# Filter coefficients by four small matmul tiles in one pair of PSUM banks, and folds issued half a step later

## The chip, the cores and the metric

The kernel runs on one core of one Trainium2 chip. The metric is the device time of one execution in microseconds (us); less is better. Five engines work side by side, each through its own queue in order: TensorE (PE; its weight loads are listed apart, as PEld), VectorE (DVE), ScalarE (ACT), GpSimd (POOL), and SyncE (SP), which here only issues DMAs. They wait for each other through semaphores.

## The reference

A long convolution by FFT gates the tokens, and two feed-forward layers follow:

```python
h_mlp = np.maximum(pos_emb @ w1, 0.0) @ w2          # filter: S x 64 -> 64 -> 128
u = x * v
h_filt = h_mlp * np.exp(-0.01 * pos)[:, None]
y = irfft(rfft(u, 2 * S) * rfft(h_filt, 2 * S))[:S]  # S = 12480, 128 channels
t = x * y
t = np.maximum(t @ moe_w_in, 0) ** 2 @ moe_w_out     # 128 -> 2048 -> 128
h = t @ moe2_w_in
out = (np.maximum(h, 0) + alpha * np.minimum(h, 0)) @ moe2_w_out
```

The change touches only how the filter's second layer (`@ w2`) is applied in the frequency domain and when its results are used.

## The kernel before, in words

The transform of length L = 110 x 229 is done as two small dense transforms, 110 points (`dfa`) and 229 points folded to 115 rows (`dfb`). The stages follow each other in program order, and a round-robin of Python generators (`run`) decides how two of them interleave. The order on each engine is the order in which this code issues.

- `z_stage`, `ar_stage`: first filter layer and its 110-point transform, kept in `ar` with 64 hidden features per frequency.
- `r_stage` with `u_stage(0)`: the 229-point transform of the 64 hidden features gives `r` tiles. One `r` tile is [128, 2, 4, 115]: on the 128 partitions lie 64 features of each of two frequencies, and it holds four frequencies in all (`q` = pair, then four combinations of real/imaginary and sign). Beside it, the first 64 channels of the signal are transformed into `U(0)`.
- **First half of the products** (`p_stage(0)`, 14 steps n = 0 to 13) beside `u_stage(1)`, which transforms the other 64 channels: `u_mm_a` (L312, 16 recorded passes per group of channels), `u_mm_b` (L320 to L325, 8 passes), and the **folds** (L328, two DVE instructions that add and subtract the two parts `pe` and `t`). `t` is an ACT copy of `po` (L324).
- **Second half of the products** (`p_stage(1)`, n = 14 to 27) beside `b_stage(0)`, the inverse transform of the first half (L409 on PE, L413 on ACT).
- Then `b_stage(1)`, `y_stage` (L466: inverse 110-point transform; two tiles of 64 output channels side by side in the array), and the two feed-forward layers, from about 313 us to the end.

One **step** n of `p_stage` does, for four frequencies: `filters(n, c)` for c = 0 (real) and c = 1 (imaginary): four matmuls each (L363) of the 128-partition `r` tile with a 128 x 128 block matrix `w2_sb` in which half of the entries are zero, so that both frequencies of a pair come out of one matmul. Each result has a bank of its own in turn (`r_h`, two banks). DVE multiplies it with U into A and then into B (L386; called **A** and **B** below). Then A is completed by a subtraction and an addition (L396, two instructions, on DVE, but on POOL in the steps of `on_pool` = 2, 6, 10, 15, 18, 21, 24, where B lies in SBUF and not in the PSUM tile `wide`), and POOL folds the result back into U (`finish`, L357). With two banks, PE may compute the next `filters(n + 1, 0)` as soon as A of step n has been read.

An fp32 matmul appears in the trace as two PE records, here called **passes**.

Of the kernel before, what the change touches and what calls it, by code (L numbers as in the profile page):

```python
# [58 lines left out]
def kernel(  # L59
# [18 lines left out]
    idft_o: bass.AP,  # L78
    out: bass.AP,
# [10 lines left out]
    six = [psum.tile([128, 512], F32, name=f"bank{i}") for i in range(6)]  # L90
    s_pair = ctx.enter_context(ExitStack())

    def last_two(name, *sizes):
        s_pair.close()
        pool = s_pair.enter_context(tc.tile_pool(name=name, bufs=1, space=PSUM))
        return [pool.tile([128, n], F32, name=f"{name}{i}") for i, n in enumerate(sizes)]

    banks = six + last_two("pair", 512, 512)
    r_any, r_six, r_a, r_b, r_h = Ring(banks), Ring(six), Ring(banks[0:2]), Ring(banks[2:5]), Ring(banks[5:8])
# [61 lines left out]
    def load_first(pool):  # L161
# [13 lines left out]
        nc.sync.dma_start(out=sig_sb, in_=sign)  # L175
        nc.sync.dma_start(out=dfa, in_=dft_a)
        load(3)
# [35 lines left out]
    def ar_stage():  # L213
# [7 lines left out]
        for c in range(F // 4):  # L221
            f0 = 4 * c
            p = [bank(r_six, HB, 4, K2) for s in range(2)]
            for s in range(2):
                for j in range(4):
                    nc.tensor.matmul(p[s][:, j], lhsT=rv[:, f0 + j, s], rhs=dfa[:, s * K2:(s + 1) * K2])  # L226
# [88 lines left out]
    def u_mm_b(k):  # L315
# [11 lines left out]
        for s, op in enumerate((ALU.add, ALU.subtract)):  # L327
            nc.vector.tensor_tensor(out=u[:, :, s], in0=pe, in1=t, op=op)  # L328
# [18 lines left out]
    def p_stage(h, t_ring, r_ring):  # L347
# [11 lines left out]
        def filters(n, c):  # L359
            H = bank(r_h, HB, DH, 2, 2, 2)  # L360
            for q in range(2):
                for s in range(2):
                    nc.tensor.matmul(  # L363
                        H[:, :, s, q], lhsT=r_t[p_order[n]][:, q, 2 * s + c], rhs=w2_sb[:, h * D:(h + 1) * D]
                    )
            return H

        first = []
        if h:
            first += [filters(nj, c) for c in range(2)]  # L370
            yield
        for n in range(h * nj, (h + 1) * nj):
# [379 lines left out]
    with tc.manual_schedule():  # L752
# [10 lines left out]
        with ExitStack() as st:  # L763
            late = st.enter_context(tc.tile_pool(name="late", bufs=1, side="right"))
            w2_sb = late.tile([128, 2 * D], F32, name="w2_sb")
# [3 lines left out]
            with tc.tile_pool(name="early", bufs=1) as early:  # L769
                run((z_stage(*load_first(early)), 1))  # L770
# [13 lines left out]
            (wide,) = last_two("wide", 1024)  # L784
            r_b.items, r_h.items, r_ab.items = six[2:4], six[4:6], six[0:4]
# [9 lines left out]
        banks = six + last_two("pair", 512, 512)  # L795
        r_y.items = six
# [87 lines left out]
def _tables(cell):  # L884
# [9 lines left out]
    ic[0] *= 0.5  # L894
    dft_b = np.zeros((HB, 3, HX), f)
# [8 lines left out]
    return w[cell].astype(f), dft_a, dft_b, e.astype(f), np.stack([o, -o], 1).astype(f)  # L904


def _arrays(inp):
    n, live, starts, order = _cells()
    cell, sign = _pairs(n, live)
    win, dft_a, dft_b, e, o = _tables(cell)  # L910
# [15 lines left out]
    w2 = np.zeros((2, F, 2, DH, 2), inp["w2"].dtype)  # L926
    for i in range(2):
        w1[i, :, i] = inp["w1"]
        w2[i, :, :, :, i] = inp["w2"].reshape(F, 2, DH)
# [34 lines left out]
```

## Time and profile before

| | us |
|---|---|
| time before, median of 3 runs (1384.39 to 1384.77) | 1384.49 |
| the profiled execution's own time | 1384.36 |
| its span, first to last instruction | 1382.6 |
| first half of the products (DVE's first A to its last B) | 119.1 to 186.5 |
| second half of the products | 195.2 to 241.1 |
| granted TensorE clock, mean over the span | 1.000 |

Over the whole span PE is recorded busy 99%, DVE 83%, POOL 74%, ACT 71%. PE's records overlap (they are modelled from issue to end), so what one pass costs is read from the distance of starts: the chain of waits gives it, as the time of a row divided by its count.

### The profile page before, as it was taken

What the parts mean: (1) busy time and instruction counts of PE and PEld (TensorE: products, weight loads), DVE (VectorE), ACT (ScalarE), POOL (GpSimd) and SP (SyncE); (2) the same over time, 40 slices, a digit from 0 to 9 for tenths busy, and PEclk for the clock granted to TensorE, in tenths of its full rate; (3) what the DMA queues carried; (4) which work ended last, traced back from release to release, by engine and by line L of the source; (5) the groups of instructions that cost most, each with busy time, mean ns of one, the idle gap of its engine ahead of it and who ended that gap; (6) DMA issues with size and microseconds to landing.
All of it is one profiled execution on the core that took longest, in us unless ns stands there. A gap on an engine that the chain in (4) does not pass through costs nothing.

```text
span 1382.6 us, 23568 instructions
## 1 busy us (share of the span) xinstructions
PE 1374.7 (99%) x8036; PEld 1193.9 (86%) x8036; DVE 1146.6 (83%) x1806; ACT 984.4 (71%) x1863; POOL 1029.3 (74%) x857
## 2 busy tenths in 40 slices
PE   9999999999999999999999999999999999999998
PEld 9999999998888888888888888888888888888898
DVE  6888989867888888888888878888888878888888
ACT  4453333638887777877777787778777787778777
POOL 4955969577877777777777777777777777777777
PEclk9999999999999999999999999999999999999999
DMA  8666423574000000000000000000000000000000
GB/s 250 185 199 186 129 65 114 157 245 146 31 2 0 9 9 1 8 9 8 9 9 9 8 1 9 9 8 8 9 8 1 9 8 8 9 9 9 1 8 19
DMA packets 59020, 66.27 MB, mean 48 GB/s; under 512 B 6226, under 2 KB 48019, under 8 KB 58771
## 3 DMA queue, kind: packets, MB, share of 16 engines
q1 hardware_dynamic: 58490, 64.56, 15.2%
q8 instruction: 63, 1.03, 0.3%
q14 instruction: 58, 0.48, 0.1%
q10 hardware_dynamic: 409, 0.21, 0.1%
HBM read 47.83 MB, written 16.92 MB: 47 GB/s over the span
## 4 chain that ended last, share of the span: by engine, by line
PE 96%; DVE 2%; issue 1%; POOL 1%; ACT 0%; POOLq 0%; DVEq 0%; ACTq 0%
PE bank L637 19%; PE bank L638 19%; PE bank L639 19%; PE pair L638 6%; PE pair L639 6%; PE pair L637 6%; PE bank L409 3%; PE bank L466 3%; PE bank L363 3%; PE bank L286 2%; PE bank L226 2%; PE bank L312 2%; PE bank L299 1%; PE pair L245 1%; PE bank L191 1%
## 5 line engine op out<-in xcount | busy, mean ns | idle before, releaser
L690 POOL TENSOR_TENSOR g<-R,g 128x512 fp32r<-128x512 f32 (+1 forms) x601 | 779.6, 1314 | 257.9 <-ACT g L679 243.7
L672 DVE SCALAR_TENSOR_TENSOR R<-bank,e 128x512 f32<-128x512 f32 (+1 forms) x800 | 530.8, 674 | 137.0 <-POOL g L690 99.2
L679 ACT CAST g<-R 128x512 fp32r<-128x512 f32 (+1 forms) x800 | 469.6, 605 | 76.6 <-DVE R L672 69.2
L657 ACT ACTIVATE e<-bank 128x512 f32<-128x512 f32 (+1 forms) x400 | 234.9, 587 | 104.0 <-PE bank L639 101.3
L662 DVE TENSOR_SCALAR e<-bank,alpha 128x512 f32<-128x512 f32 (+1 forms) x266 | 195.2, 734 | 35.9 <-PE bank L639 34.6
L690 DVE TENSOR_TENSOR g<-R,g 128x512 fp32r<-128x512 f32 (+1 forms) x199 | 185.0, 930 | 0.0
L638 PE MATMUL pair<-g,w_o 128*128 128x512 f32 (+1 forms) x400 | 153.7, 384 | 0.4 <-POOL g L690 0.4
L637 PE MATMUL bank<-x,w_i 128*128 128x512 f32 (+1 forms) x400 | 153.8, 385 | 0.0
L637 PE MATMUL pair<-g,w_o 128*128 128x512 f32 (+1 forms) x400 | 153.7, 384 | 0.0
L638 PE MATMUL bank<-x,w_i 128*128 128x512 f32 (+1 forms) x400 | 153.6, 384 | 0.0
L639 PE MATMUL bank<-x,w_i 128*128 128x512 f32 (+1 forms) x400 | 153.5, 384 | 0.0
L639 PE MATMUL pair<-g,w_o 128*128 128x512 f32 (+1 forms) x400 | 153.5, 384 | 0.0
L637 PE MATMUL bank<-g,w_o0b 128*128 128x512 f32 (+1 forms) x350 | 134.4, 384 | 0.0
L638 PE MATMUL bank<-g,w_o0b 128*128 128x512 f32 (+1 forms) x350 | 134.4, 384 | 0.0
L639 PE MATMUL bank<-g,w_o0b 128*128 128x512 f32 (+1 forms) x350 | 134.3, 384 | 0.0
L659 ACT ACTIVATE e<-bank 128x512 f32<-128x512 f32 (+1 forms) x134 | 78.8, 588 | 34.1 <-PE bank L639 32.5
L660 ACT ACTIVATE e<-e,alpha 128x512 f32<-128x512 f32 (+1 forms) x134 | 95.5, 713 | 4.4
L637 PEld LDWEIGHTS bank<-x,w_i 128*128 128x128 f32 x400 | 75.1, 188 | 15.0 <-DVE R L672 0.9
L638 PEld LDWEIGHTS pair<-g,w_o 128*128 128x128 f32 x400 | 75.1, 188 | 14.7 <-POOL g L690 1.0
L639 PEld LDWEIGHTS bank<-x,w_i 128*128 128x128 f32 x400 | 75.1, 188 | 14.4
L639 PEld LDWEIGHTS pair<-g,w_o 128*128 128x128 f32 x400 | 75.1, 188 | 14.4
L638 PEld LDWEIGHTS bank<-x,w_i 128*128 128x128 f32 x400 | 75.3, 188 | 13.8
(138 smaller groups left out, 2531.9 us busy)
## 6 DMA issues: line engine op xcount, KB each, us to landing
r<-spill SPq DMA_DIRECT2D x22, 460.0 KB, 3.3
G<-in_xs_dram SPq DMA_DIRECT2D x32, 224.0 KB, 3.8
G<-in_vs_dram SPq DMA_DIRECT2D x32, 224.0 KB, 3.7
spill<-r SPq DMA_DIRECT2D x14, 460.0 KB, 3.0
out_dram<-R SPq DMA_DIRECT2D x23, 256.0 KB, 2.0
s_w<-in_moe_w_out_dram SPq DMA_DIRECT2D x16, 256.0 KB, 5.3
s_w<-in_moe_w_in_dram SPq DMA_DIRECT2D x16, 256.0 KB, 2.9
w_spill<-w_o SPq DMA_DIRECT2D x15, 256.0 KB, 4.2
```

The costliest lines, as they stand in the source:

```text
L363: nc.tensor.matmul(H[:, :, s, q], lhsT=r_t[p_order[n]][:, q, 2 * s + c], rhs=w2_sb[:, h * D:(h + 1) * D])
L409: nc.tensor.matmul(p[:, d], lhsT=U(h, 2 * (x0 + d) + e, 1)[:, 0], rhs=icosb if e == 0 else isinb)
L637: nc.tensor.matmul(p, lhsT=wl, rhs=xh, start=first, stop=False)
L638: nc.tensor.matmul(p, lhsT=wh, rhs=xl, start=False, stop=False)
L639: nc.tensor.matmul(p, lhsT=wh, rhs=xh, start=False, stop=last)
L657: nc.scalar.activation(out=r, in_=p, func=ACTF.Relu)
L659: nc.scalar.activation(out=r, in_=p, func=ACTF.Relu, scale=-1.0)
L660: nc.scalar.activation(out=r, in_=r, func=ACTF.Copy, scale=alpha[:, t:t + 1])
L662: nc.vector.tensor_scalar(out=r, in0=p, scalar1=0.0, scalar2=alpha[:, t:t + 1], op0=ALU.min, op1=ALU.mult)
L672: nc.vector.scalar_tensor_tensor(out=g, in0=p, scalar=0.0, in1=r, op0=ALU.max, op1=op)
L679: nc.scalar.copy(out=gh, in_=g)
L690: eng.tensor_tensor(out=gl, in0=g, in1=gh.bitcast(F32), op=ALU.subtract)
```

## The change

**Filters.** `w2_sb` holds the 64 x 128 matrix twice, once per half of the partitions, with no zeros. Each old matmul (128 rows, 115 columns of weights, 128 moving columns) becomes four: 64 rows (one frequency of the pair), 64 or 51 columns of weights (the 115 output rows cut at 64), 64 moving columns. A step has 32 of them instead of 8, all issued together in `filters(n)`. The results of a step, both c, lie in one tile `filt` of two banks, one bank per frequency of the pair. `filt` exists once: `filters(n + 1)` is issued after A and B of step n, and writes where they read.

**Reading.** DVE reads `filt` with a step of 256 elements between the four frequencies of a channel (before: four neighbours). PE writes every second element. To give the pairs the right members, the 110-point transform of the filter has its own table `dff` with permuted columns, loaded early, with the first signal loads ahead of `dfa`.

**Folds.** `u_mm_b` returns its folds, and `u_stage` issues them after the next `u_mm_a`. The counts given to `run` change a little.

**Banks.** Four fixed PSUM banks and four regrouped ones instead of six and two.

```diff
-        def filters(n, c):
-            H = bank(r_h, HB, DH, 2, 2, 2)
+        def filters(n):
+            k, w = n // nj * DH, r_t[p_order[n]]
+            H = filt.rearrange("p (r q c d s) -> p r q c d s", r=2, q=2, c=2, s=2)
             for q in range(2):
                 for s in range(2):
-                    nc.tensor.matmul(
-                        H[:, :, s, q], lhsT=r_t[p_order[n]][:, q, 2 * s + c], rhs=w2_sb[:, h * D:(h + 1) * D]
-                    )
-            return H
-
-        first = []
-        if h:
-            first += [filters(nj, c) for c in range(2)]
-            yield
+                    for c in range(2):
+                        for r in range(2):
+                            f = slice(F * r, F * r + F)
+                            for b in (slice(0, 64), slice(64, HB)):
+                                nc.tensor.matmul(H[b, r, q, c, :, s], lhsT=w[f, q, 2 * s + c, b], rhs=w2_sb[f, k:k + DH])
+
+        hv = filt[:HB].rearrange("p (k c x) -> p c x k", k=4, c=2)
+        if not h:
+            filters(0)
...
             for c, out_c in enumerate((A, B)):
-                H = first.pop(0) if first else filters(n, c)
-                hv = H.rearrange("p d s q r -> p (d s) (q r)")
...
-                        in1=hv[:, x0:x0 + m].unsqueeze(2).to_broadcast([HB, m, 2, 4]),
+                        in1=hv[:, c, x0:x0 + m].unsqueeze(2).to_broadcast([HB, m, 2, 4]),
...
                 if c == 0:
                     yield
+            if n + 1 < 2 * nj:
+                filters(n + 1)
             for c, op in ((0, ALU.subtract), (1, ALU.add)):
...
     def u_stage(h, parts=None):
+        folds = None
         for k in range(h * NG, (h + 1) * NG + 1):
             if k < (h + 1) * NG:
                 prep(min(k + NV - 3, loaded[0] - 1))
                 load(k + NV - 1)
                 u_mm_a3(k, parts) if parts else u_mm_a(k)
+            if folds:
+                folds()
+            if k < (h + 1) * NG:
                 yield
             if k > h * NG:
-                u_mm_b3(k - 1) if parts else u_mm_b(k - 1)
+                folds = u_mm_b3(k - 1) if parts else u_mm_b(k - 1)
+                if folds and k == (h + 1) * NG:
+                    folds()
                 yield
...
-            run((some(u, 2 * NG - 1), 2 * NG), (p0, 2 * nj + 3))
-            next(q0)
+            run((some(u, 2 * NG - 1), 2 * NG), (p0, 2 * nj + 1))
             next(u)
             next(back)
-            run((b_stage(0, False), NG), (q0, 2 * nj + 3))
+            run((b_stage(0, False), NG), (q0, 2 * nj + 2))
```

Before, PE in the second half, `bank_73` and `bank_74` being the two filter banks and `bank_69` to `bank_72` those of the inverse transform:

```order
L363 MATMUL bank_73<-w_sb,r_112 115x64x2 x4
L363 MATMUL bank_74<-w_sb,r_112 115x64x2 x4
L409 MATMUL bank_71<-dfb,G 112x116 x4
L409 MATMUL bank_72<-dfb,G 112x116 x4
L363 MATMUL bank_73<-w_sb,r_110 115x64x2 x4
```

The same place now, where `wide_1134` is the tile `filt`:

```order
L422 MATMUL bank_70<-dfb,G 112x116 x4
L380 MATMUL wide_1134<-w_sb,r_112 64x64
L380 MATMUL wide_1134<-w_sb,r_112 51x64
...
L422 MATMUL bank_71<-dfb,G 112x116 x4
L422 MATMUL bank_72<-dfb,G 112x116 x4
```

The two groups of four became one run of 32, of which the first matmul waits for DVE and the rest for nothing.

Before, DVE at the start of the first half (`T` is A, or both A and B in an `on_pool` step; L328 are the folds), steps 1 to 3:

```order
L328 TENSOR_TENSOR R_82<-bank_71,G 115x4x112 x2
L386 TENSOR_TENSOR T_1137<-G,bank_73 115x128
L386 TENSOR_TENSOR T_1137<-G,bank_73 115x896
L386 TENSOR_TENSOR wide_1132<-G,bank_74 115x128
L386 TENSOR_TENSOR wide_1132<-G,bank_74 115x896
L396 TENSOR_TENSOR T_1137<-T_1137,wide_1132 115x128x4 x2
L328 TENSOR_TENSOR R_82<-bank_71,G 115x4x112 x2
L386 TENSOR_TENSOR T_1139<-G,bank_73 115x128
```

The same place now (`wide_1135` is the old `wide`):

```order
L397 TENSOR_TENSOR T_1140<-G,wide_1134 115x128
L397 TENSOR_TENSOR T_1140<-G,wide_1134 115x896
L332 TENSOR_TENSOR R_82<-bank_71,G 115x4x112 x2
L397 TENSOR_TENSOR wide_1135<-G,wide_1134 115x128
L397 TENSOR_TENSOR wide_1135<-G,wide_1134 115x896
L409 TENSOR_TENSOR T_1140<-T_1140,wide_1135 115x128x4 x2
L397 TENSOR_TENSOR T_1142<-G,wide_1134 115x128
```

The folds moved from behind L396 to between A and B; that is so in steps 1 to 4 and 10 to 13. In steps 4 to 9 a pair of folds stands behind B (and L396), as before.

Before, DVE in the second half:

```order
L386 TENSOR_TENSOR T_1136<-R_82,bank_73 115x1024
L386 TENSOR_TENSOR wide_1132<-R_82,bank_74 115x1024
L396 TENSOR_TENSOR T_1136<-T_1136,wide_1132 115x128x4 x2
L386 TENSOR_TENSOR T_1137<-R_82,bank_73 115x1024
L386 TENSOR_TENSOR wide_1132<-R_82,bank_74 115x1024
```

The same place now:

```order
L397 TENSOR_TENSOR T_1139<-R_82,wide_1134 115x1024
L397 TENSOR_TENSOR wide_1135<-R_82,wide_1134 115x1024
L409 TENSOR_TENSOR T_1139<-T_1139,wide_1135 115x128x4 x2
L397 TENSOR_TENSOR T_1140<-R_82,wide_1134 115x1024
L397 TENSOR_TENSOR wide_1135<-R_82,wide_1134 115x1024
```

The order is the same; what moved is the bank: every multiplication reads the one tile `wide_1134`.

## Rows read from the trace of the kernel before

**Rows 1.** Windows of the span: start:end, length, busy of engines (instructions), clock, DMA
```profile
118.20:188.90 70.70, 70.31 (x579) 68.76 (x577) 64.35 (x106) 24.00 (x45) 60.19 (x75) 1.00 0.43 128
193.50:243.30 49.80, 48.68 (x466) 48.26 (x464) 47.08 (x52) 17.63 (x33) 42.05 (x34) 1.00 0.39 118
```

**Rows 2.** Chain that ended last: start, length, what; one step of the first half
```profile
169.49 0.88 PE bank L363 x8
170.37 0.38 PE bank L320 x2
170.75 0.38 PE bank L321 x2
171.13 0.38 PE bank L322 x2
171.50 0.38 PE bank L325 x2
171.88 0.87 PE bank L363 x8
172.76 1.61 PE bank L312 x16
```

**Rows 3.** The same chain: a step of the second half, a handover to DVE, the stage behind
```profile
203.87 1.75 PE bank L363 x16
205.62 1.59 PE bank L409 x16
...
231.46 0.03 issue
231.48 0.02 DVEq L386
231.50 0.04 issue
...
243.29 25.61 PE bank L409 x256
```

**Rows 4.** Windows, DVE alone: first half, between the halves, second half
```profile
119.10:186.50 67.40, 61.99 (x102) 1.00 0.44 130
186.50:195.10 8.60, 4.70 (x9) 1.00 0.19 56
195.10:241.10 46.00, 43.78 (x46) 1.00 0.36 106
```

**Rows 5.** Timeline of DVE: start, length, line; two places of the first half
```profile
125.35 1.27 DVE L386 TENSOR_TENSOR T<-G,bank 115x128 f32<-115x128 f32 x2
126.54 1.42 DVE L386 TENSOR_TENSOR wide<-G,bank 115x128 f32<-115x128 f32 x2
127.99 1.29 DVE L396 TENSOR_TENSOR T<-T,wide 115x512 f32<-115x512 f32 x2
129.20 1.15 DVE L328 TENSOR_TENSOR R<-bank,G 115x448 f32<-115x448 f32 x2
130.26 2.47 DVE L386 TENSOR_TENSOR T<-G,bank 115x128 f32<-115x128 f32 x4
133.13 1.16 DVE L328 TENSOR_TENSOR R<-bank,G 115x448 f32<-115x448 f32 x2 [0.39 <-ACT G L324]
```

**Rows 6.** Timeline of DVE: one step of the second half
```profile
195.16 1.22 DVE L386 TENSOR_TENSOR T<-R,bank 115x1024 f32<-115x1024 f32 x1
196.30 1.22 DVE L386 TENSOR_TENSOR wide<-R,bank 115x1024 f32<-115x1024 f32 x1
197.55 1.29 DVE L396 TENSOR_TENSOR T<-T,wide 115x512 f32<-115x512 f32 x2
198.75 2.35 DVE L386 TENSOR_TENSOR T<-R,bank 115x1024 f32<-115x1024 f32 x2
```

**Rows 7.** PE's filter passes: two bursts on the timeline, the first one held up by DVE
```profile
200.13 2.16 PE L363 MATMUL bank<-w_sb,r 128*115 128x128 f32 x16
...
203.71 1.91 PE L363 MATMUL bank<-w_sb,r 128*115 128x128 f32 x16
```

**Rows 8.** PE in the y stage, window of L466 alone: length, busy (passes)
```profile
271.00:311.00 40.00, 40.00 (x852) 1.00 0.81 252
```

**Rows 9.** Timeline of PE at the start of the y stage
```profile
269.13 0.83 PE L445 MATMUL bank<-w_i 128*128 128x112 f32 x6
269.90 0.33 PE L466 MATMUL bank<-ide,G 112*64 112x55 f32 x4
270.06 0.31 PE L466 MATMUL bank<-ido,G 112*64 112x55 f32 x3
270.18 0.27 PE L466 MATMUL bank<-ide,G 112*64 112x110 f32 x1
270.21 0.22 PE L466 MATMUL bank<-ido,G 112*64 112x55 f32 x1
```

**Rows 10.** Groups by line: count, busy us, mean ns, idle before; ACT's copy, DVE's strided read
```profile
L324 ACT COPY G<-bank 115x448 f32<-115x448 f32 x14 | 7.5, 533 | 20.6 <-PE bank L322 20.6
...
L228 DVE COPY R<-bank 115x448 f32<-115x448 f32 x16 | 10.0, 624 | 4.4 <-PE bank L226 4.2
...
L328 DVE TENSOR_TENSOR R<-bank,G 115x448 f32<-115x448 f32 x32 | 18.4, 617 | 4.9 <-ACT G L324 4.9
```

More of the change, by code (lines that the diff above doesn't have):

```diff
@@ L78 @@
     idft_o: bass.AP,
+    dft_f: bass.AP,
     out: bass.AP,
@@ L89, with last_four @@
     psum = ctx.enter_context(tc.tile_pool(name="psum", bufs=1, space=PSUM))
[L90 to L95, printed above, removed]
+    four = [psum.tile([128, 512], F32, name=f"bank{i}") for i in range(4)]
+    s_four = ctx.enter_context(ExitStack())
+    def last_four(name, *sizes):
+        s_four.close()
+        pool = s_four.enter_context(tc.tile_pool(name=name, bufs=1, space=PSUM))
         return [pool.tile([128, n], F32, name=f"{name}{i}") for i, n in enumerate(sizes)]
-    banks = six + last_two("pair", 512, 512)
-    r_any, r_six, r_a, r_b, r_h = Ring(banks), Ring(six), Ring(banks[0:2]), Ring(banks[2:5]), Ring(banks[5:8])
+    banks = four + last_four("lone", 512, 512, 512, 512)
+    r_any, r_six, r_a, r_b, r_h = Ring(banks), Ring(banks[:6]), Ring(banks[0:2]), Ring(banks[2:5]), Ring(banks[5:8])
     r_ab, r_y = Ring([]), Ring([])
@@ L175, in load_first @@
         nc.sync.dma_start(out=sig_sb, in_=sign)
+        nc.sync.dma_start(out=dff, in_=dft_f)
+        load(3)
         nc.sync.dma_start(out=dfa, in_=dft_a)
-        load(3)
         nc.sync.dma_start(out=dfb, in_=dft_b)
@@ L225, in ar_stage @@
                 for j in range(4):
-                    nc.tensor.matmul(p[s][:, j], lhsT=rv[:, f0 + j, s], rhs=dfa[:, s * K2:(s + 1) * K2])
+                    nc.tensor.matmul(p[s][:, j], lhsT=rv[:, f0 + j, s], rhs=dff[:, s])
             for s, copy in enumerate((nc.scalar.copy, nc.vector.tensor_copy)):
@@ L326, in u_mm_b, with folds @@
         u = U(h, 2 * DG * g, 2 * DG).rearrange("p (d s) (c k) -> p d s c k", s=2, c=2)
-        for s, op in enumerate((ALU.add, ALU.subtract)):
-            nc.vector.tensor_tensor(out=u[:, :, s], in0=pe, in1=t, op=op)
+        def folds():
+            for s, op in enumerate((ALU.add, ALU.subtract)):
+                nc.vector.tensor_tensor(out=u[:, :, s], in0=pe, in1=t, op=op)
+        return folds
     def u_stage(h, parts=None):
+        folds = None
         for k in range(h * NG, (h + 1) * NG + 1):
@@ L764 @@
             late = st.enter_context(tc.tile_pool(name="late", bufs=1, side="right"))
-            w2_sb = late.tile([128, 2 * D], F32, name="w2_sb")
+            w2_sb = late.tile([128, D], F32, name="w2_sb")
             dfa = late.tile([NA, 2 * K2 + KA], F32, name="dfa")
@@ L769 @@
             with tc.tile_pool(name="early", bufs=1) as early:
+                dff = early.tile([NA, 2, K2], F32, name="dff")
                 run((z_stage(*load_first(early)), 1))
@@ L789 @@
             u = u_stage(1)
-            run((some(u, 2 * NG - 1), 2 * NG), (p0, 2 * nj + 3))
-            next(q0)
+            run((some(u, 2 * NG - 1), 2 * NG), (p0, 2 * nj + 1))
             next(u)
             next(back)
-            run((b_stage(0, False), NG), (q0, 2 * nj + 3))
-        banks = six + last_two("pair", 512, 512)
-        r_y.items = six
+            run((b_stage(0, False), NG), (q0, 2 * nj + 2))
+        banks = four + last_four("apart", 512, 512, 512, 512)
+        r_y.items = banks[:6]
         wa = ctx.enter_context(tc.tile_pool(name="wa", bufs=1))
@@ L941, in _arrays @@
         arrays[k] = a.view(np.int64) if a.dtype.itemsize == 8 else a
-    arrays.update(win=win, sign=sign, dft_a=dft_a, dft_b=dft_b, idft_e=e, idft_o=o)
+    arrays.update(win=win, sign=sign, dft_a=dft_a, dft_b=dft_b, idft_e=e, idft_o=o, dft_f=dft_f)
     return arrays, starts, order
```

14 lines of the change are left out of this document (7 added, 7 removed).

## Prediction

> **What bounds the kernel now.** I read the windows of the two halves of the products first. In both PE is busy all the time and DVE nearly so: 64.35 of 70.7 us and 47.08 of 49.8 us [rows 1]. The chain of waits runs over PE in both, and its rows give the price of a step. First half: 0.88 + 1.52 + 0.87 + 1.61 = 4.88 us, of which 1.75 are the 16 filter passes [rows 2]. Second half: 1.75 + 1.59 = 3.34 us [rows 3]. Then I read DVE's timeline for its price of the same step. First half: A 1.19 (start to start), B 1.45, L396 1.21, folds 1.06, together 4.91 us, or 3.70 where L396 lies on POOL [rows 5]. Second half: A and B 2.39, L396 1.20, together 3.59 [rows 6]; without L396 some 2.36. So PE and DVE are within a few per cent of each other, and what lets both run is that each has something in hand: with a bank for each of the two results, PE computes the next filters while DVE still multiplies. DVE is idle for only 67.40 - 61.99 = 5.4 us in the first half and 46.00 - 43.78 = 2.2 us in the second [rows 4]. Behind the products PE alone is the bound (25.61 us of L409 without a gap [rows 3], then the y stage and the layers), so a delay of the products reaches the end undiminished.
>
> **What a burst of 32 small matmuls takes.** No row shows a tile of 64 rows and 64 columns. One pass by itself is bounded by its weights or its moving columns: L312 takes 1.61/16 = 101 ns for 115 weight columns (0.875 ns each), L363 1.75/16 = 109 ns for 128 moving columns (0.855 ns each) [rows 2, 3]. For 64 and 64 that is 55 to 56 ns; I take 58, with 2 ns for the handing over. A step has 64 passes, 16 on each of the four tiles. If the tiles work side by side, the burst takes 16 x 0.058 = 0.93 us; if nothing overlaps, 64 x 0.058 = 3.7 us. The nearest row is the y stage, with two tiles of 64 columns: 852 passes in 40 us are 46.9 ns each [rows 8], while one of 110 moving columns needs 94 ns, so both tiles work at full rate. I take 0.93 us: a gain for PE of 0.8 us per step, 23 us over 28 steps.
>
> **What it does to the path.** The gain falls on an engine that no longer sets the end. The burst of step n + 1 may start only when B of step n has been read, and A of step n + 1 only when the whole burst is done. From the end of B to the next A, DVE cannot multiply for a time G:
> - PE's restart after a wait: the burst that DVE held up took 2.16 us, the next one 1.91 [rows 7]: 0.25.
> - Fifteen passes to the start of the last one: 15 x 0.058 = 0.87.
> - The record of the last pass, some 0.24 (0.22 to 0.27 in the y stage [rows 9]), and 0.09 until DVE runs [rows 3].
>
> G = 1.46 us (0.25 of the restart may shrink, so 1.2 to 1.5). Only L396 and folds can fill it.
>
> Second half: each of 14 steps takes 2.39 + 1.46 = 3.85 us; L396 (1.20) fits into G where it is on DVE, and nothing fills it in the four steps where it is on POOL. From the first A to the last B: 13 x 3.85 + 2.36 = 52.4 us, against 241.1 - 195.2 = 45.9: **+6.5 us**. PE needs only 1.59 + 0.93 + 0.3 of the 3.85.
>
> First half: DVE's work is the same, so I count its idle time. Behind steps 0, 1, 3, 11, 12 stands L396 alone: 5 x (1.46 - 1.21) = 1.25. Behind steps 2 and 10 (on POOL) nothing: 2.92. Behind step 6 a pair of folds: 0.40. Behind 5, 7, 8, 9 L396 and folds, 2.27: nothing. The moved folds cost, too. In eight steps they stand between A and B, and they need `u_mm_b`, which on PE now stands behind the burst: after the start of the burst's last pass (1.12 after B) come its stream and a change of the array's shape, 0.15 (L466 starts 0.20 after the last L445, whose passes are 0.11 apart [rows 9]), three matmuls of 0.38 [rows 2], 0.2 for the record's end and the signal, ACT's copy 0.53 [rows 10] and 0.1: 3.25 us after B. A is through at 1.46 + 1.19 = 2.65, so DVE waits 0.6 each time: 4.8. Behind step 4 the fold stands in the gap itself and waits for the same chain: 3.25 - 1.21 = 2.0. Together 11.4, less the 5.4 of before: **+6.0 us**. Before, such folds waited at times (0.39 [rows 5]).
>
> Between the halves DVE idles 8.60 - 4.70 = 3.9 us now [rows 4], waiting for the last folds; the two that remain there wait 2.0 and some 1.8: nothing. The first A waits for a burst of 0.93 instead of one of 0.88, plus a change of shape: +0.2.
>
> Edits taken at nothing: the stride of DVE's reads (L228 reads a bank at a stride of 112 elements in 624 ns, the folds neighbours in 617 [rows 10]; 7 ns on 56 multiplications would be 0.4 us), the two PSUM splits (the same number of banks in every ring outside the products), `dff` (smaller than `dfa`, in its place; `dfa` is first used behind the whole `ar` stage, which hides its later load), POOL (its work is unchanged, and a longer step gives it more room), `w2` (half the bytes). PE's writes at every second element have no row; if they slowed a pass to the old 109 ns, the burst would take 1.75 us, which is the first rival's price.
>
> Sum: 6.5 + 6.0 + 0.2 = 12.7 us. Against the profiled execution, 1384.36 (0.1 below the median), this gives **1397 us**.
>
> **Rivals.**
> 1. *Two tiles at a time.* The two passes of an fp32 matmul go to the same tile one behind the other, so if PE starts passes strictly in order, the next tile can overlap only with the second pass: the burst takes 64 x 0.058 / 2 = 1.86 us, and G 2.39. Second half 13 x 4.78 + 2.36 = 64.5 (+18.6). First half 5 x 1.18 + 4.8 + 1.33 + 2.9 + 0.5 + 4.8 = 20.2 (+14.8). With the 0.2 and a longer first burst +34, 1418 us. Against it: at the start of the y stage a 110-column pass of the next group starts at 270.18, ahead of a 55-column pass of the group before at 270.21 [rows 9], so tiles run out of order. For it: only two tiles were ever seen. The Trainium skill states the order as a rule ("TensorE: Matmul & The Clock Gate", Part 3, What overlaps and what doesn't: matmuls start and end strictly in program order); the row just named disagrees, by 0.03 us at one place. The same page (Part 1, on the 56 ns) gives a floor of about 25 ns from start to start; by an estimate from it, 64 passes take 1.6 us, and the time would be some 1412; no run here shows passes closer than 46.9 ns on average.
> 2. *The tiles do not overlap at all*, and the change only adds passes: burst 3.7 us, G 4.2. Second half 13 x 6.6 + 2.4 = 88 (+42), first half +39: 1466 us. The y stage speaks against it.
> 3. *A shorter burst.* If both passes of a matmul overlapped as well, or weights of 64 rows loaded faster, the burst were some 0.45 us and G 0.98, less than L396. Second half 9 x 3.59 + 4 x 3.37 + 2.4 = 48 (+2.3), first half 2.0 + 1.5 + 4.8 - 5.4 (+2.9): 1390 us. No row has a pass below its columns' price.
> 4. *Not slower: the multiplications get shorter.* They read the filters from two banks instead of one (L386, now L397); if that made them faster, 56 of them pay for 12.7 us at 0.23 us each (of some 1.2), and at 0.18 the change is within 0.2%: 1384 to 1387. L228 and the folds, one strided and one not, read at the same rate, so there is no sign of it.
>
> **How the numbers follow.** Forecast (1393 to 1402, with G from 1.25 to 1.65): 0.61. Two at a time, or a floor between (1405 to 1423): 0.23. No overlap: 0.05. Short burst (1388 to 1391): 0.06. Shorter multiplications: 0.05. The range that leaves out no more than 2 in 10 runs from 1389 to 1421. About 0.2% (2.8 us) is what a measurement of this kernel can tell from no change. Slower by more: 0.61 + 0.23 + 0.05 + 0.06, less 0.02 for short bursts that end within it: 0.93. Within: 0.05. Faster: 0.02.
>
> **What would show it.** The window of the second half: PE's share falls to some 70%, and DVE's idle time grows from 2.2 to 8 or 9 us, put down to PE's filter line; the distance from one A to the next is 3.85 us in steps with and without L396 alike. Passes of the filter line: 64 in about 0.93 us (1.86 in the first rival, 3.7 in the second). In the first half DVE's folds wait for ACT in steps 1 to 4 and 10 to 13. The y stage starts some 13 us later than 269.9, and from there all is as before. The forecast is wrong if A of the next step starts less than 1.2 us after B where L396 is on POOL, if multiplications no longer take 1.2 us, or if the stages before 118 us or behind 313 us change their length.

## The result, and the profile of the changed kernel

The changed kernel takes **1396.71 us** (median of 4 runs, 1395.81 to 1397.09), the kernel before 1384.47 beside it on the same chip: a ratio of 1.0088, 95% interval 1.0073 to 1.0102. It is slower by about 12 us. Its profiled execution took 1397.09 us, with a span of 1395.3.

The windows of after that answer to [rows 1, 4], from the first A to the last B of a half and of the time between (columns: start:end, length, then busy us and instructions of PE, PE's weight loads, DVE, ACT, POOL, then the granted clock, DMA share and GB/s):

```profile
120.54:195.22 74.68, 62.85 (x1184) 57.61 (x1184) 64.02 (x104) 23.42 (x44) 59.29 (x72) 1.00 0.40 118
195.22:202.53 7.31, 6.42 (x96) 5.38 (x96) 3.60 (x7) 1.06 (x2) 2.76 (x4) 1.00 0.18 64
202.53:253.90 51.37, 40.36 (x1067) 37.32 (x1067) 44.58 (x46) 16.25 (x30) 41.91 (x34) 1.00 0.33 96
```

The first half grew from 67.40 to 74.68 us, the second from 46.00 to 51.37; between them 8.60 became 7.31. PE is now idle for 11.8 us in the first and 11.0 in the second, where it was busy nearly all the time, and DVE's idle time grew too: 10.7 us instead of 5.4, and 6.8 instead of 2.2. The two engines, which had worked at the same time throughout, now work by turns for the length of each burst.

DVE's timeline in the second half (start, length, line; in brackets its idle time before and what ended it) beside [rows 6]:

```profile
203.66 1.22 DVE L397 TENSOR_TENSOR wide<-R,wide 115x1024 f32<-115x1024 f32 x1
204.92 1.29 DVE L409 TENSOR_TENSOR T<-T,wide 115x512 f32<-115x512 f32 x2
206.24 2.35 DVE L397 TENSOR_TENSOR T<-R,wide 115x1024 f32<-115x1024 f32 x2
209.94 1.22 DVE L397 TENSOR_TENSOR T<-R,wide 115x1024 f32<-115x1024 f32 x1 [1.35 <-PE wide L380]
```

and PE's in the same place:

```profile
204.94 1.15 PE L380 MATMUL wide<-w_sb,r 64*64 64x64 f32 x64 [2.36 <-DVE wide L397]
206.03 1.84 PE L422 MATMUL bank<-dfb,G 115*112 115x116 f32 x16
208.65 1.16 PE L380 MATMUL wide<-w_sb,r 64*64 64x64 f32 x64 [0.78 <-DVE T L397]
```

B of a step ends at 204.88, PE starts the burst at 204.94, and the next A starts at 206.24: the gap is 1.36 us, and L409 lies in it from 204.92 to 206.21. At 208.59 the same gap stands bare, because L409 lies on POOL: 1.35 us idle, put down to PE's filter line L380. A follows A after 3.71 us in both cases (202.53, 206.24, 209.94), with L409 or without. Before, it was 3.59 with it and 2.36 without.

In the first half a step looks like this on DVE, where [rows 5] had the folds behind L396:

```profile
124.45 1.28 DVE L397 TENSOR_TENSOR T<-G,wide 115x128 f32<-115x128 f32 x2
126.34 1.16 DVE L332 TENSOR_TENSOR R<-bank,G 115x448 f32<-115x448 f32 x2 [0.61 <-ACT G L326]
127.42 1.42 DVE L397 TENSOR_TENSOR wide<-G,wide 115x128 f32<-115x128 f32 x2
128.87 1.29 DVE L409 TENSOR_TENSOR T<-T,wide 115x512 f32<-115x512 f32 x2
130.12 1.29 DVE L397 TENSOR_TENSOR T<-G,wide 115x128 f32<-115x128 f32 x2
```

The folds stand between A and B and wait 0.61 us for ACT's copy. A step takes 5.67 us instead of 4.91. The view of the waits from 117 to 275 us adds it up (us, times, longest):

```profile
DVE T L397 <- PE wide L380: 10.9, 8, 2.1
DVE R L332 <- ACT G L326: 10.1, 11, 1.9
```

From the last B to the y stage nothing changed. It starts 28.81 us after it in both, at 282.69 us (PE's timeline, below) instead of 269.90 [rows 9]:

```profile
282.69 0.33 PE L479 MATMUL apart<-ide,G 112*64 112x55 f32 x4
```

### The profile page after: what moved, and what is told of

It is laid out like the page before. It is cut to its first block, busy times and chain, and to the rows that moved or that the text cites. A ratio compares the mean times of both kernels' runs of the same rounds, so it can differ in the third digit from the quotient of the medians.

```text
span 1395.3 us, 26237 instructions
## 1 busy us (share of the span) xinstructions
PE 1362.8 (98%) x9380; PEld 1174.2 (84%) x9380; DVE 1147.2 (82%) x1806; ACT 983.2 (70%) x1863; POOL 1028.7 (74%) x857
## 4 chain that ended last, share of the span: by engine, by line
PE 91%; DVE 6%; issue 1%; ACT 1%; POOL 1%; DMA 0%; SPq 0%; POOLq 0%; ACTq 0%; DVEq 0%
PE bank L650 13%; PE bank L651 13%; PE bank L652 13%; PE apart L650 13%; PE apart L651 13%; PE apart L652 12%; DVE T L397 2%; PE bank L479 2%; DVE wide L397 2%; PE bank L288 2%; PE lone L247 2%; PE bank L422 2%; PE wide L380 1%; PE bank L228 1%; DVE R L332 1%; DVE T L409 1%
## 5 line engine op out<-in xcount | busy, mean ns | idle before, releaser
L651 PE MATMUL apart<-g,w_o 128*128 128x512 f32 (+1 forms) x400 | 153.7, 384 | 0.4 <-POOL g L703 0.4
L650 PE MATMUL bank<-x,w_i 128*128 128x512 f32 (+1 forms) x400 | 153.8, 385 | 0.0
L650 PE MATMUL apart<-g,w_o 128*128 128x512 f32 (+1 forms) x400 | 153.7, 384 | 0.0
L652 PE MATMUL apart<-g,w_o 128*128 128x512 f32 (+1 forms) x400 | 153.5, 384 | 0.0
L650 PE MATMUL apart<-g,w_o0b 128*128 128x512 f32 (+1 forms) x350 | 134.4, 384 | 0.0
L651 PE MATMUL apart<-g,w_o0b 128*128 128x512 f32 (+1 forms) x350 | 134.4, 384 | 0.0
L652 PE MATMUL apart<-g,w_o0b 128*128 128x512 f32 (+1 forms) x350 | 134.3, 384 | 0.0
L651 PEld LDWEIGHTS apart<-g,w_o 128*128 128x128 f32 x400 | 75.1, 188 | 14.7 <-POOL g L703 1.0
L652 PEld LDWEIGHTS apart<-g,w_o 128*128 128x128 f32 x400 | 75.1, 188 | 14.5
```

What stands on the lines that cost most here:

```text
L650: nc.tensor.matmul(p, lhsT=wl, rhs=xh, start=first, stop=False)
L651: nc.tensor.matmul(p, lhsT=wh, rhs=xl, start=False, stop=False)
L652: nc.tensor.matmul(p, lhsT=wh, rhs=xh, start=False, stop=last)
```

## The experiments

Times are compared with runs of the kernel before on the same chip (1384.3 to 1384.6 us). All but one start from the changed kernel or from one another. Of each edit the lines that matter are shown; `...` marks what is left out. The question of the first seven is what the 12 us are made of; of the other five, whether the loss belongs to the small tiles or only to the place of their burst, and what is left of the change when the burst is out of the way.

**The fold move, undone.** In `u_mm_b`, the folds are issued at once:

```diff
-        return folds
+        folds()
```

> The changed kernel with the folds of u_mm_b issued at once again, as before the change; tiles, banks and the place of the filter bursts stay. Theory: on PE the three u_mm_b matmuls now stand behind the burst, so the folds are ready only some 3.25 us after B; placed at once they stand ahead of the next A, and DVE waits for the whole chain in the gap (3.25 + 1.06 us) where after waits 1.36 and then 0.6 between A and B: some 1.3 to 1.7 us more in each of 13 steps of the first half, 1413 to 1420 us, second half unchanged (51.35 us from first A to last B). Rival: the moved folds are themselves a cost (the 4.8 us of waits in the middle of eight steps), and undoing them gives some 1390 to 1393. A move worth nothing gives 1396.7.

Measured: 1428.2 us (1426.9 to 1431.83), ratio 1.0319 (1.0304 to 1.0335). DVE's timeline, an early and a late place, and the window between:

```profile
125.25 1.16 DVE L332 TENSOR_TENSOR R<-bank,G 115x448 f32<-115x448 f32 x2 [1.86 <-ACT G L326]
132.07 1.16 DVE L332 TENSOR_TENSOR R<-bank,G 115x448 f32<-115x448 f32 x2 [1.81 <-ACT G L326]
200.85 1.16 DVE L332 TENSOR_TENSOR R<-bank,G 115x448 f32<-115x448 f32 x2 [6.38 <-ACT G L326]
```
```profile
180.00:190.00 10.00, 7.19 (x89) 6.65 (x88) 5.03 (x8) 1.57 (x3) 2.76 (x4) 0.66 0.16 49
```

In the early steps the mechanism is as expected: the folds start 3.17 us after B (forecast of the chain: 3.25), and a step takes 6.8 us, 1.15 more than in the changed kernel, a little less than the 1.3 to 1.7 expected. If all 13 steps lost as much, that would be some 15 us. The total is above the range because of something not foreseen: PE's waits grew, its granted clock fell (0.66 in this window, with stretches at 1.2 GHz between 158.5 and 199.5 us), and the matmuls that DVE waits for became slower in turn. So the moved folds are no cost of the change; without them the new place of the burst would have cost some 31 us more, part of it through PE's clock. The rival falls.

**The fold move alone**, put into the kernel before.

> The kernel before with the fold move alone: filters as before (whole 128 x 128 matmuls, a bank for each result). Theory: the folds waited little before (4.9 us in all, for ACT), and half a step later they wait no more than that, so 1383 to 1387 us. Rival: folds between A and B delay B and so the whole step, the 4.8 us forecast for the first half come from the place of the folds and not from the burst ahead of them: 1389 to 1391.

Measured: 1385.09 us, ratio 1.0004 (0.9995 to 1.0013): no difference. The folds' group (count, busy us, mean ns, idle before) answers to the last line of [rows 10]:

```profile
L330 DVE TENSOR_TENSOR R<-bank,G 115x448 f32<-115x448 f32 x32 | 18.4, 618 | 3.8 <-ACT G L324 3.8
```

They wait 3.8 us in all, not 10.1. The place between A and B is harmless by itself; the 0.6 us come from the burst that now stands ahead of `u_mm_b` on PE.

**The old matmuls in the new place.** Eight matmuls of 128 rows, all behind B, into the one pair of banks:

```diff
...
             for q in range(2):
                 for s in range(2):
+                    for c in (1, 0):
+                        nc.tensor.matmul(H[:HB, c, :, s, q], lhsT=w[:, q, 2 * s + c], rhs=w2_sb[:, k:k + D])
...
-                    nc.tensor.matmul(p[s][:, j], lhsT=rv[:, f0 + j, s], rhs=dff[:, s])
+                    nc.tensor.matmul(p[s][:, j], lhsT=rv[:, f0 + j, s], rhs=dfa[:, s * K2:(s + 1) * K2])
```

> The changed kernel with the old eight matmuls of 128 rows and their zero blocks, but in the new place: all eight behind B, into the one pair of banks that both A and B read; fold move kept. Theory: the loss comes from the single buffer, and its size is the burst's length. A burst of 1.75 instead of 0.94 us makes the gap some 0.8 us longer in all 13 steps of the second half (51.35 becomes 61 to 62 us) and in 7 to 13 of the first: 1413 to 1418 us. Rival: the loss comes from the small tiles (four times as many matmuls, changes of the array's shape, writes at every second element), and the old matmuls bring it back: 1384 to 1390.

Measured: 1420.75 us, ratio 1.0262 (1.0247 to 1.0277). The second half takes 61.56 us, as expected. A burst on PE, the bare gap on DVE, and one row from the start of the program:

```profile
226.87 2.00 PE L377 MATMUL wide<-w_sb,r 128*115 128x128 f32 x16 [0.94 <-DVE wide L394]
```
```profile
224.45 1.22 DVE L394 TENSOR_TENSOR T<-R,wide 115x1024 f32<-115x1024 f32 x1 [2.17 <-PE wide L377]
```
```profile
22.04 4.18 PE L228 MATMUL bank<-dfa,G 110*115 110x112 f32 x20 [4.02 <-DMA dfa<-in_dft_a_dram]
```

The old matmuls do not bring the time back; they make the gap 2.17 us. So the loss is the single buffer's, and the small tiles make it smaller. The last row was not expected: this kernel takes `dfa` for the `ar` stage while `dfa` is loaded behind the signals, and PE waits 4.02 us for it; the 20 passes behind the wait take 4.18 us, at a granted clock of 0.50. The first A is at 125.88 us instead of 120.54. That is why the time ends above its range, and it shows that the table of the `ar` stage (`dff` in the changed kernel) is needed ahead of the signals.

**The burst twice.** The same 32 matmuls issued a second time:

```diff
             if n + 1 < 2 * nj:
                 filters(n + 1)
+                filters(n + 1)
```

> The changed kernel with every burst behind a B issued twice: the 32 small matmuls, and the same 32 again, writing the same filters. Theory: what costs is the burst's length between B and the next A, whatever it is made of. 64 more passes are 0.94 us more: the gap goes from 1.35 to 2.3 us, the second half from 51.35 to 63 to 64 us, the first by some 8 us (it grew by 6.9 with the whole matmuls, whose burst was 0.79 us longer): 1417 to 1422 us. Rival: a burst has a fixed price besides its passes (the change of the array's shape, the restart), so that much of the 1.35 us stays and the second 32 matmuls add clearly less than 0.94 us each time: 1405 to 1412.

Measured: 1424.29 us, ratio 1.0286 (1.0270 to 1.0301). PE's burst and DVE's bare gap:

```profile
223.40 2.09 PE L380 MATMUL wide<-w_sb,r 64*64 64x64 f32 x128 [0.79 <-DVE T L397]
```
```profile
225.63 1.22 DVE L397 TENSOR_TENSOR T<-R,wide 115x1024 f32<-115x1024 f32 x1 [2.29 <-PE wide L380]
```

The gap grew by 0.94 us, as much as the burst's row (2.09 instead of 1.16): passes are paid in full. Some 0.4 us of the 1.35 are not paid per pass; they are the start of the burst behind B (0.06), the record of the last pass (0.22) and the time until DVE starts (0.13). Both halves grew by more than forecast, and the time ends above its range. The first took 12.0 us more (0.92 per step), since PE with 2.1 + 1.6 + 1.7 us a step is now later than DVE in the steps that had cover too (from the burst behind step 5 to that behind step 9, one follows another after 5.3 to 5.7 us). The second took 15.4 more, 12.2 of them in 13 gaps; the rest goes with a stretch at a clock of 0.50, from 217.0 to 220.4 us (mean of the half 0.97).

**The order of the tiles.** The 32 matmuls with one tile's eight in a row (first edit), and with the two tiles of the same 64 rows in turn (second); only the new loops are shown, without the matmul in them:

```diff
+            for r in range(2):
+                f = slice(F * r, F * r + F)
+                for b in (slice(0, 64), slice(64, HB)):
+                    for q in range(2):
+                        for s in range(2):
+                            for c in range(2):
...
```
```diff
+            for r in range(2):
+                f = slice(F * r, F * r + F)
+                for q in range(2):
+                    for s in range(2):
+                        for c in range(2):
+                            for b in (slice(0, 64), slice(64, HB)):
...
```

> The changed kernel with the 32 matmuls of a burst in another order: the 8 of one tile in a row, then the 8 of the next, where after changes the tile with every matmul. Same matmuls, same banks. Theory 1: every tile has a queue deep enough for 16 passes, the four still run side by side: burst 0.94 to 1.1 us, 1396 to 1399 us. Theory 2: PE looks only a few passes ahead, tiles overlap only where their passes stand next to each other in the program: burst some 3.5 us instead of 0.94, some 2.5 us more per step in the second half and about as much in the first: 1440 to 1465 us.

> The changed kernel with the 32 matmuls in a third order: 16 that alternate between the two tiles of the upper 64 rows, then 16 that alternate between the two of the lower. Theory: two tiles run side by side as long as their matmuls stand in turn, so the burst takes 32 x 0.058 = 1.86 us, little less if the two groups overlap where they meet; the gap is the burst and 0.4 us, 2.2 us; about the price of burst_twice without its slower clock, 1414 to 1421 us. Rival: neighbours of the same 64 rows hinder each other as much as one tile's own matmuls do, burst above 2.5 us as with one tile after the other: above 1430.

Measured: 1474.87 us (1470.08 to 1478.37), ratio 1.0661, and 1428.65 (1422.33 to 1436.43), ratio 1.0321 (1.0281 to 1.0362). PE's row of the first kernel at full clock and DVE's gap behind it, then two of PE's rows of the second, the earlier one from a stretch at half clock, DVE's gap behind the later one, and a window of that stretch:

```profile
269.61 3.32 PE L380 MATMUL wide<-w_sb,r 64*64 64x64 f32 x64 [0.74 <-DVE T L397]
```
```profile
273.04 1.22 DVE L397 TENSOR_TENSOR T<-R,wide 115x1024 f32<-115x1024 f32 x1 [3.48 <-PE wide L380]
```
```profile
225.60 3.31 PE L380 MATMUL wide<-w_sb,r 64*64 64x64 f32 x64
...
279.86 1.90 PE L380 MATMUL wide<-w_sb,r 64*64 64x64 f32 x64 [0.76 <-DVE T L397]
```
```profile
281.89 1.22 DVE L397 TENSOR_TENSOR T<-R,wide 115x1024 f32<-115x1024 f32 x1 [2.08 <-PE wide L380]
```
```profile
220.00:250.00 30.00, 30.00 (x383) 28.57 (x379) 13.95 (x16) 4.36 (x8) 17.36 (x14) 0.50 0.22 67
```

At full clock the same matmuls take 1.16, 1.90 or 3.32 us, depending only on which tile the next one goes to. One tile after the other, 64 passes start within 3.10 us, nearly one after the other: in the burst shown the second tile's first pass starts at 270.37, when only three of the first tile's sixteen are still to come (270.42 to 270.54). So PE does start passes ahead of program order, which the first rival denied, but here only about three passes ahead. It does not reach the next tile behind sixteen passes of one, and tiles run side by side only if their matmuls stand next to each other. The change wrote them in an order that allows it. Both kernels end above their ranges, since they lost time beyond the burst, to PE's clock: the first has a mean of 0.91 in the first half and 0.87 in the second, the second kernel 0.50 in all of the window shown. The lower the mean clock of an execution of the second, the longer it took: 1422 us at 0.993, 1435 at 0.980.

With these runs the bare gap can be set beside the burst (PE's row in the timeline, DVE's idle time in a step with L409 on POOL, all at full clock):

| kernel | burst, us | gap, us |
|---|---|---|
| after | 1.16 | 1.35 |
| two tiles in turn | 1.90 | 2.08 |
| whole tiles | 2.00 | 2.17 |
| burst twice | 2.09 | 2.29 |
| tile after tile | 3.32 | 3.48 |

The gap is the burst's row plus 0.16 to 0.20 us, whatever the burst is made of.

**The early loads.** `dfa` is loaded ahead of `load(3)` again:

```diff
-        load(3)
         nc.sync.dma_start(out=dfa, in_=dft_a)
+        load(3)
```

> The changed kernel with the table dfa loaded ahead of load(3) again, as in the kernel before; the new table dff stays behind sign. Theory: the first stage's 1.17 us more in the changed kernel's profiled execution come from the order of these loads, and go: its last pass at 17.5 to 17.9 us instead of 18.87, the time 0.5 to 1.2 us below 1396.7. Rival: they are the spread of that stage from one execution to the next (17.4 to 18.8 us in the runs so far, with the same loads), and the time stays within 0.5 us of 1396.7.

Measured: 1396.06 us (1395.71 to 1397.31), ratio 1.0086 (1.0072 to 1.0100). Last passes of the first stage in this kernel, and in the changed one:

```profile
17.23 0.60 PE L193 MATMUL lone<-w_sb,G 128*110 128x128 f32 x4
```
```profile
18.54 0.60 PE L193 MATMUL lone<-w_sb,G 128*110 128x128 f32 x4
```

The stage ended 1.3 us earlier here, but the median is only 0.65 below, and the runs overlap. Seven other kernels with the changed order of loads start their last pass of this stage between 17.54 and 18.79 us, the kernel before at 17.70. The 1.17 us of the changed kernel's profiled execution lie within this spread; whether the order has a share of a few tenths stays open.

**The folds one half step later still**, behind the next B, into the gap (`due` holds the folds that `u_stage` got from `u_mm_b` and has not issued yet):

```diff
...
                 if c == 0:
                     yield
+            while due:
+                due.pop(0)()
             if n + 1 < 2 * nj:
                 filters(n + 1)
```

> The changed kernel with the folds put off by one more half step: behind the next B instead of between A and B, ahead of L409, so that they stand in the gap in which DVE waits for the burst. Tiles, banks and PE's order stay. Theory: the first half lost by waiting for the folds between A and B (0.54 to 0.61 us in most steps, 1.86 and 1.21 in two) and by a gap of 1.35 that only L409 filled; with the folds (1.06, ready long before) in the gap, L409 and folds are longer than the gap, and DVE waits only where L409 lies on POOL: first half 74.7 becomes 64 to 67 us, second half stays at 51.35: 1385 to 1389 us. Rival: u_mm_b on PE must wait until the folds have read its two banks, and gives back what DVE gains: 1392 to 1397.

Measured: 1387.59 us (1385.95 to 1388.52), ratio 1.0022 (1.0013 to 1.0031). A step on DVE, and PE's burst in it:

```profile
125.54 1.42 DVE L400 TENSOR_TENSOR wide<-G,wide 115x128 f32<-115x128 f32 x2
126.87 1.15 DVE L332 TENSOR_TENSOR R<-bank,G 115x448 f32<-115x448 f32 x2
127.94 1.27 DVE L414 TENSOR_TENSOR T<-T,wide 115x512 f32<-115x512 f32 x2
129.13 2.47 DVE L400 TENSOR_TENSOR T<-G,wide 115x128 f32<-115x128 f32 x4
```
```profile
127.50 1.16 PE L383 MATMUL wide<-w_sb,r 64*64 64x64 f32 x64
```

No idle time is left in such a step: folds and L414 (2.2 us) cover the burst. Where L414 lies on POOL, 0.53 us remain. The first half takes 65.26 us, less than before the change; the second is still 51.33. Three quarters of the loss are gone by moving the folds once more.

**And two pairs of filter banks in the second half.** `b_stage` gets two banks, the two that `u_mm_b` had become the other pair, and each burst is issued a step ahead:

```diff
...
+            hv = buf(n)[:HB].rearrange("p (k c x) -> p c x k", k=4, c=2)
+            if h and n + 1 < 2 * nj:
+                filters(n + 1)
...
-            if n + 1 < 2 * nj:
+            if not h:
                 filters(n + 1)
```

> folds_behind_b, and in the second half the filters alternate between two pairs of banks: the pair that u_mm_b used in the first half holds every other step's filters, b_stage has two banks instead of four, and each burst is issued a step ahead, before A of the step in front of it. Theory: with the burst out of the gap nothing stands between B and the next A but L409, and the second half becomes DVE's own work, 9 x 3.59 + 4 x 2.39 + 2.4 = 44.3 us, at most 46 instead of 51.35: 1378 to 1383 us, faster than before. Rival: b_stage with two banks waits for ACT's copies, PE becomes late and the second half stays above 49 us: 1384 to 1388.

Measured: 1381.6 us (1381.01 to 1383.54), ratio 0.9982 (0.9973 to 0.9991): faster than both. The second half takes 43.73 us. But the y stage now starts 32.65 us behind the last B instead of 28.81. PE's rows there, and the window:

```profile
239.52 3.40 PE L434 MATMUL bank<-dfb,R 115*112 115x116 f32 x16 [3.17 <-DVE R L374]
```
```profile
240.00:244.00 4.00, 4.00 (x23) 4.00 (x22) 0.15 (x1) 1.40 (x3) 0.00 (x0) 0.50 0.00 0
```

16 passes take 3.40 us where they took 1.75: after 3.17 us without work PE runs at 1.2 GHz, and in this execution the gain is partly given back. It took 1383.54 us, the longest of the 11, so the others may have lost less there.

**And 12 matmuls that nobody reads**, in that idle time:

```diff
+            fill = bank(r_ab, K2, DG, HX)
+            for d in range(12):
+                nc.tensor.matmul(fill[:, d % DG], lhsT=dfb[:, 0, :K2], rhs=dfb[:, 2])
```

> second_half_two_buffers with 12 matmuls more, whose result nobody reads, on PE behind the last b_stage of the first set and ahead of the first of the second. There PE waited 3.17 us for DVE's last sums, and its granted clock was 0.50 for some 6 us after that, 193 ns from one pass to the next instead of 99. Theory: the idle time in front costs the clock; 12 matmuls of two passes of some 0.1 us fill 2.4 to 2.5 of the 3.17 us, the clock stays at 1.00, and the y stage starts some 3 us earlier behind the last B: 1377.5 to 1380 us. Rival: the clock falls for another reason, or the filler delays what comes behind it as much as it saves: 1381 to 1383.

Measured: **1379.76 us** (1379.59 to 1379.99), ratio 0.9966 (0.9953 to 0.9978), the fastest of all, 4.9 us below the kernel before. PE, and the window of the second half:

```profile
235.13 2.63 PE L823 MATMUL bank<-dfb 115*112 115x116 f32 x24
238.45 1.81 PE L434 MATMUL bank<-dfb,R 115*112 115x116 f32 x16 [0.69 <-DVE R L374]
```
```profile
191.80:235.54 43.74, 41.35 (x1077) 38.56 (x1077) 43.43 (x46) 16.99 (x32) 39.66 (x33) 1.00 0.44 133
```

The filler runs, 0.69 us of idle time remain, the clock stays at 1.00, the 16 passes take 1.81 us, and the y stage starts 29.53 us behind the last B. By the medians, each against the kernel before on its chip, the filler is worth some 2 us. DVE is busy for 43.43 of 43.74 us: the second half is its own work.

**The same with the old whole matmuls**, to see what the small tiles are worth in this order:

```diff
...
-                                nc.tensor.matmul(H[b, r, q, c, :, s], lhsT=w[f, q, 2 * s + c, b], rhs=w2_sb[f, k:k + DH])
+                        nc.tensor.matmul(H[:HB, c, :, s, q], lhsT=w[:, q, 2 * s + c], rhs=w2_sb[:, k:k + D])
```

> two_buffers_and_filler with the old eight matmuls of 128 rows, in the same places and banks; the tables are loaded in the same order, with dff's columns not permuted. It tells what the small tiles are worth once their burst is off the path. Theory: they are worth PE's 0.8 us per step wherever PE is the later engine: first half 1.73 + 0.25 + 1.5 + 1.6 = 5.1 us on PE against DVE's 4.91, second half 1.73 + 0.1 + 1.6 = 3.4 to 3.5 against 3.59 and 2.39, so the first half takes 69 to 72 us instead of 65.3, the second 45 to 47 instead of 43.7: 1385 to 1390 us. Rival: with the burst off the path its length no longer matters, the banks did all of it: 1379 to 1382.

Measured: 1388.51 us, ratio 1.0030 (1.0018 to 1.0043). Its two halves:

```profile
119.64:189.72 70.08, 68.47 (x558) 66.33 (x557) 61.98 (x103) 22.68 (x43) 59.03 (x72) 1.00 0.41 123
197.78:242.81 45.03, 45.03 (x432) 45.00 (x432) 43.67 (x46) 15.60 (x29) 40.96 (x34) 1.00 0.39 113
```

The time and both halves are where the theory had them. PE is busy nearly all the time and is the later engine again. The small tiles are worth some 9 us here (4.9 us below the kernel before with them, 4.2 above it without); in the changed kernel the same tiles stood in a place that cost 12.

**A pair of banks for each result**, with B's result in SBUF instead of PSUM, the folds issued at once and the y stage's tables loaded later:

```diff
...
-            B = t_ring() if apart else wide[:HB].rearrange("p (x c k) -> p x c k", k=4, c=2)
-            A = t_ring()
+            A, B = t_ring(), t_ring()
```

> Small tiles with a pair of banks for each of the two results, as the kernel before had a bank for each: filters of A are computed while B is multiplied, and those of B while A is. The two banks come from B's result, which lies in SBUF instead of PSUM (the ring there holds five such tiles), folds at once, and the two tables of the y stage are loaded behind the products. Theory: without the single buffer the gap is gone and the small tiles' shorter burst is all that is left: 1380 to 1387 us. Rival: the five tiles are too few, DVE waits for POOL's sums of two steps earlier, or DVE's sum of two SBUF tiles beside POOL is slower than 1.2 us: above 1390.

Measured: 1402.53 us, ratio 1.0132 (1.0118 to 1.0146). The rival holds, by its second branch. The sums on DVE, and POOL beside them:

```profile
206.18 1.29 DVE L405 TENSOR_TENSOR T<-T,T 115x512 f32<-115x512 f32 x2
...
212.04 2.69 DVE L405 TENSOR_TENSOR T<-T,T 115x512 f32<-115x512 f32 x2
```
```profile
207.56 2.49 POOL L365 TENSOR_TENSOR R<-T 115x512 f32<-115x512 f32 x2 [7.76 <-DVE T L405]
209.99 2.52 POOL L405 TENSOR_TENSOR T<-T,T 115x512 f32<-115x512 f32 x2
212.59 3.25 POOL L365 TENSOR_TENSOR R<-T 115x512 f32<-115x512 f32 x2
```

At 206.18 POOL is idle, and two sums take 1.29 us; at 212.04 POOL works, and they take 2.69. All sums of this kernel on DVE (count, then shortest, median and longest, ns), and those of the changed kernel, where B lies in PSUM:

```profile
L405 DVE TENSOR_TENSOR T<-T,T x42: 676/1004/2208, 123.4 to 258.3; 115x512 f32<-115x512 f32 x42
```
```profile
L409 DVE TENSOR_TENSOR T<-T,wide x42: 678/684/689, 123.2 to 254.5; 115x512 f32<-115x512 f32 x42
```

The sums that have no instruction of POOL beside them take 676 to 692 ns; every one above 700 has, and ends some 0.55 us after a POOL instruction beside it has ended. The idle time at the gap did go, but DVE's own work grew: 71.70 busy us in the first half instead of 64.02, and 53.34 instead of 44.58 in the second. PE's granted clock is 0.96 on average in the first half (0.50 from 153.8 to 160.7 us); what that adds there was not separated.

## Why the prediction was right, point by point

The forecast was 1397 us, a sum of 12.7; measured were 1396.71 and, between the profiled executions, 12.73. The mechanism held: a gain on an engine that did not set the end, paid for with a buffer that did. That the sum agrees so closely is partly luck, since two errors cancel.

- *The burst.* Forecast 16 x 0.058 = 0.93 us, of which 0.87 from the first to the last start; measured are 0.937 from the first to the last start, in all 28. Two passes of one tile start 56 to 58 ns apart, as forecast, but the first of a tile stands some 0.10 us ahead of its second, which the forecast did not have. The writes at every second element cost nothing that shows in the 58 ns.
- *G.* Forecast 1.46 (its terms add up to 1.45), measured 1.35 to 1.36. The restart was put at 0.25; in the rows the burst starts 0.06 us behind B's end, and the 0.07 that the starts in it take over the forecast are there in bursts that did not wait, too. The last record is 0.22 (forecast 0.24), and the handover to DVE, put at 0.09, takes 0.13.
- *Second half.* Forecast +6.5, measured +5.4, with 3.71 us from A to A instead of 3.85. The difference is 0.14 in each of 13 steps, less 0.74 for one gap of 2.09 us, where two groups of `b_stage` stood ahead of one burst; this was not forecast. DVE's idle time grew to 6.8 us, not to the 8 or 9 expected. PE's share was put at some 70% and is 79% (40.36 of 51.37): the forecast counted starts, 1.59 and 0.93 us, where PE's rows of the two groups, with the last record's end, are 1.84 and 1.16.
- *First half and between.* Forecast +6.0 and nothing, measured +7.3 and -1.3, which is the same sum: one pair of folds (1.06 us) now falls into the half and no longer behind it. Folds between A and B wait 0.54 to 0.61 in six of the eight steps (forecast 0.6), behind step 4 1.86 (forecast 2.0). Steps 10 and 11 were missed: the folds wait 1.21 and 0.18 there, and the bare gap behind step 10 is 1.71. DVE's idle time in the half grew by 5.3 us, where 6.0 was forecast.
- *First A.* From the last pass of the first stage to the first A it takes 0.24 us more; forecast 0.2.
- *Edits at nothing.* The multiplications take 1220 and 1222 ns (1216 and 1223 before), so the stride costs nothing that shows and the fourth rival falls. The forecast also had the stages before 118 us unchanged. In the profiled execution they ended 1.17 us late, which fills the place of the 1.1 us that the second half came out short. By the runs above this is mostly spread from one execution to the next; an execution of nearly the same kernel without it took 1395.71.
- *Rivals.* Two tiles at a time was priced at 1418 us with a burst of 1.86; the kernel in which PE really runs two at a time has a burst of 1.69 from first to last start and took 1422 in the executions less hit by the clock. No overlap was priced at 1466; tile after tile took 1475, with a shorter burst (3.10 instead of 3.7) and a lower clock. Both prices were near, in part by luck, since the measured times hold a loss to the clock that the prices had not; and what brings either about is the order of the matmuls, which the prediction didn't see as something that the code decides. The strict program order of the first rival is not what PE does: see the burst of tile after tile above. A floor that would stretch the burst to 1.6 us did not show, and a shorter burst did not occur.
- *What the prediction didn't ask* is whether the fold move helps. Undone, it costs 31 us, part of them through PE's clock, and half a step more would have saved another 9.

## What to carry to other kernels

Before making an engine's burst shorter, look at where it stands: between two steps of another engine its whole length is paid each time, plus about 0.2 us here, except for what that engine can do meanwhile; and half the length in the wrong place was dearer here than the full length beside other work. Put what is already computed (here the folds) into such a gap before asking for another buffer, then look for banks that a stage no longer needs. And let matmuls of different tiles alternate one by one.

## What the runs showed of the hardware

- Four fp32 tiles of 64 rows and 64 columns (two of them with 51 weight columns) run fully side by side if their matmuls alternate: 64 passes start within 0.94 us, 15 ns apart on average. This is below the floor of about 25 ns from start to start that the Trainium skill gives ("TensorE: Matmul & The Clock Gate", Part 1, on the 56 ns); the measurement decides. With 16 passes of one tile in a row it takes 3.10 us.
- A DVE sum of two SBUF tiles waits while POOL works: 676 to 692 ns alone, up to 2208 beside it, and every delayed sum ends some 0.55 us after a POOL instruction does; with one operand in PSUM 678 to 689 throughout. The Trainium skill states it as an exclusive lock that an instruction holds to its end ("SBUF — State Buffer", SBUF: two separate sides); these rows agree.
- PE's granted clock falls to 0.50 (1.2 GHz) in kernels in which PE waits much, and a slower PE makes the others wait longer. It fell behind 3.17 us without work, and stayed at 1.00 with 0.69 there. But the changed kernel has an idle stretch of 2.36 us (at 204.94) with a clock of 1.00, and in the kernel with two tiles in turn one of the same length, at the same place, stands ahead of more than 30 us at 0.50. What else decides was not tried.
